# VectorE's side work ahead of both convolution taps, and the leftover gate product on VectorE, in a fused FNet mixing and gated convolution kernel

## The chip, the cores and the metric

The kernel runs on one core of a Trainium2 chip. A core has a matrix engine (TensorE, PE in the profile; its weight loads are listed as PEld), a vector engine (VectorE, DVE), an engine for functions of one operand (ScalarE, ACT), a general engine (GpSimd, POOL) and an engine that here only issues DMAs (SyncE, SP). Each runs its own list of instructions in order, and semaphores hold an instruction until what it reads or overwrites is ready. The metric is device time in microseconds (us) of one execution. Before the change three runs took 1197.53, 1198.07 and 1198.87 us; the median is 1198.07.

## What is computed

The input x has the shape (8, 3136, 256). A 2D Fourier transform over sequence and features, of which the real part is kept, is followed by a gated feed-forward layer with a three-tap convolution along the sequence:

```python
X = np.fft.fft(np.fft.fft(x, axis=1), axis=2).real      # (8, 3136, 256)
h = np.maximum(X @ w_in, 0.0)                           # (8, 3136, 1024)
hp = pad(h, 1 row of zeros at both ends of the sequence)
conv_out = sum(conv_w[k] * hp[:, k:k + S, :] for k in range(3))
gate = 1.0 / (1.0 + np.exp(-conv_out))
out = (h * gate) @ w_out                                # (8, 3136, 256)
```

All numbers are float32.

## The kernel before

**Stages.** The sequence transform of a batch is folded by symmetry on VectorE (`fold_ops`, 14 pieces per batch, L142 to L199), and multiplied with cosine and sine tables on PE in eight or nine "units" (`units`, L271 to L371). A unit has PE products into one PSUM bank, for most units a ScalarE copy of half of that bank into SBUF (`copy`, L286 for even frequencies, L305 for odd-even ones), and a `fin` on VectorE that adds and subtracts the two halves into the rows PQ of the transformed sequence (L290 and L293, L309 and L311; the units called `odd`, L321 and L323, have no copy, and their `fin` follows the PE products directly). The feature transform is merged with w_in into a matrix G, so the hidden rows come from two products of G with PQ.

**Steps.** The main loop runs over 256 steps (b, c, f): 8 batches, 4 chunks of the half sequence each, and 8 blocks of 128 hidden features. A step handles 128 features by 770 positions (832 in the last chunk of a batch), as two mirrored halves of some 385 columns. For each step there are:

- `seed`: ScalarE writes the contribution of one input feature into the PSUM tile pa.
- `products`: PE adds two products (pb, pa) of 386 to 418 columns (a third in some steps of batch 0, `triple`).
- `copies`: ScalarE copies pb to SBUF as nb (L685), in `triple` steps L680 and L682.
- `combine`: VectorE makes the hidden rows h from pa and nb (L696, two instructions, or one in `triple` steps).
- `first_tap`: ScalarE multiplies h with tap 0 into g (L702).
- `tap` 1 and 2: VectorE adds the two other taps into g, in place (L707, 128x770 or 128x832 each).
- `sigmoid`: ScalarE, two instructions on g (L720), the half for POOL first.
- `gate`: g times h, half on POOL (L727) and half on VectorE (L728). In the last chunk there are 64 more columns, left over from tiles of 128, that go into a tile `left` which two batches share; this is a third product, on POOL (L730).
- `mm2`: PE multiplies the gated tiles with w_out and adds over the eight f into the PSUM tiles po (six tiles, seven in the last chunk of odd batches, the seventh from `left`). At f = 7 ScalarE copies po out (L747) and SP stores it.

**Order.** The program order of each engine is written by hand. The loop at L893 runs cycles t = 0 to 258 and handles several steps at once: products for step t+1, `combine` and `first_tap` for step t, the two taps for step t-1, sigmoid and gate for step t-2, and `mm2` for step t-3. So step s is combined in cycle s and multiplied with w_out in cycle s+3. Work for the next batch and for loading is hung into the cycles as "side" work, by cycle and place: `first`, `act`, `dve`, `load` and `pe`. The place `dve` holds the fold pieces, the `fin` of units, parts of the conversion of the weights (L538, L539, L532, L542, up to cycle 7) and a stage of the transform of one feature (L449). The place `act` holds the units' copies and comes behind `copies` of step t+1 on ScalarE. VectorE's order in a cycle is therefore: conversion of weights where there is some (L524), combine (L696), tap 1, the `dve` side work, tap 2, gate.

A unit's PE products end in the cycle before its copy and `fin`. In batches 2 to 7 there is a unit about every four cycles, and fold pieces in other cycles; around cycles 21 to 29 units come in almost every cycle. Folding ends with batch 7's data, around cycle 190.

**Buffers.** One PSUM bank for pb, two for pa, one for the units (pd), four for po; four tiles h, five tiles g.

Of the kernel before, what the change touches and what calls it, by code (L numbers as in the profile page):

```python
# [13 lines left out]
ALU = mybir.AluOpType  # L14
# [23 lines left out]
def kernel(  # L38
# [48 lines left out]
    vt = nc.vector.tensor_tensor  # L87
    gt = nc.gpsimd.tensor_tensor
    stt = nc.vector.scalar_tensor_tensor
# [407 lines left out]
    LEFT = P // 2  # L497
# [4 lines left out]
    left = const.tile([P, NF, P], F32, name="left")  # L502
# [110 lines left out]
    cw = const.tile([P, 3, NF], F32, name="cw")  # L613
# [29 lines left out]
    def cut(s):  # L643
        b, c, f = s
        ch = chunks[c]
        return ch, ch.k1 - ch.k0, slice(f * P, (f + 1) * P)

    def seed(s):

        b, c, f = s  # L650
        ch, n, fs = cut(s)
        pa[s] = psa.tile([P, 512], F32, name="pa", tag="pa")
        act(pa[s][:, 0:n], eb[b, c], AF.Copy, scale=ge[:, f:f + 1])  # L653

    def triple(s):

        return s[0] == 0 and TRIPLE[0] <= s[1] * NF + s[2] < TRIPLE[1]

    def row_of(s):
        hs[s] = hp.tile([P, HW], F32, name="h", tag="h")  # L660
        w = chunks[s[1]].w
        if chunks[s[1]].zeros:
            nc.gpsimd.memset(hs[s][:, 0:w:w - 1], 0.0)  # L663

    def products(s):
        b, c, f = s
        ch, n, fs = cut(s)
        pb[s] = psb.tile([P, 512], F32, name="pb", tag="pb")
        mm(pb[s][:, 0:n], G[0:P - 1, 1, fs], PQ[b][1][0:P - 1, ch.k0:ch.k1], True, True)
        mm(pa[s][:, 0:n], G[:, 0, fs], PQ[b][0][:, ch.k0:ch.k1], False, not triple(s))  # L670
        if triple(s):
            mm(pa[s][:, 0:n], G[0:P - 1, 1, fs], PQ[b][1][0:P - 1, ch.k0:ch.k1], False, True)

    def copies(s):

        ch, n, fs = cut(s)
        p = pb.pop(s)
        nb[s] = nbp.tile([P, 2, HN], F32, name="nb", tag="nb")
        if triple(s):
            act(nb[s][:, 1, ch.cols], p[:, ch.cols], AF.Copy, scale=-2.0)  # L680
            row_of(s)
            act(hs[s][:, ch.front], pa[s][:, ch.fcols], AF.Relu)  # L682
        else:
            for i, cols in enumerate((ch.fcols, ch.cols)):
                act(nb[s][:, i, cols], p[:, cols], AF.Copy, scale=-1.0 if i else 1.0)  # L685

    def combine(s):

        ch, n, fs = cut(s)
        a, c = pa.pop(s), nb.pop(s)  # L690
        if not triple(s):
            row_of(s)
        h = hs[s]
        for i, (to, cols) in enumerate(((h[:, ch.front], ch.fcols), (h[:, ch.back][:, ::-1], ch.cols))):
            if i or not triple(s):
                nc.vector._custom_dve(TENSOR_ADD_SAT, out=to, in0=a[:, cols], in1=c[:, i, cols],  # L696
                                      s0=BIG, s1=0.0)

    def first_tap(s):
        n = chunks[s[1]].w - 2  # L700
        gs[s] = gp.tile([P, HW - 2], F32, name="g", tag="g")[:, 0:n]
        act(gs[s], hs[s][:, 0:n], AF.Copy, scale=cw[:, 0, s[2]:s[2] + 1])  # L702

    def tap(s, k):
        g, h, f = gs[s], hs[s], s[2]
        n = g.shape[1]
        stt(out=g, in0=h[:, k:k + n], scalar=cw[:, k, f:f + 1], in1=g, op0=ALU.mult, op1=ALU.add)  # L707

    def shares(s):

        ch = chunks[s[1]]
        w = ch.w - 2
        n = ch.rest[0] if ch.last else w
        return slice(0, n // 2), slice(n // 2, n), slice(n, w)

    def sigmoid(s):

        v, p, r = shares(s)
        for c in (slice(p.start, r.stop), v):
            act(gs[s][:, c], gs[s][:, c], AF.Sigmoid)  # L720

    def gate(s):

        b, c, f = s
        g, h = gs[s], hs.pop(s)[:, 1:]
        v, p, r = shares(s)
        gt(g[:, p], g[:, p], h[:, p], op=ALU.mult)  # L727
        vt(g[:, v], g[:, v], h[:, v], op=ALU.mult)  # L728
        if r.start < r.stop:
            gt(left[:, f, b % 2 * LEFT:(b % 2 + 1) * LEFT], g[:, r], h[:, r], op=ALU.mult)  # L730

    def mm2(s):
        b, c, f = s
        ch = chunks[c]
        tiles = [(gs[s][:, o:o + m], [(0, b, r, m)]) for o, r, m in ch.tiles]
        if ch.last and b % 2:
            tiles.append((left[:, f], [(i * LEFT, b - 1 + i, ch.rest[1], LEFT) for i in range(2)]))
        for i, (w, to) in enumerate(tiles):
            if f == 0 and i % 2 == 0:
                po[b, c, i // 2] = pso.tile([P, 2, D], F32, name="po", tag="po")  # L740
            pt = po[b, c, i // 2]
            mm(pt[:, i % 2, :], w, wout[:, f, :], f == 0 and i % 2 == 0, f == NF - 1)
            if f == NF - 1 and (i % 2 or i == len(tiles) - 1):
                del po[b, c, i // 2]
                osb = osp.tile([P, 2, D], F32, name="os", tag="os")
                for j in range(i - i % 2, i + 1):
                    nc.scalar.copy(out=osb[:, j % 2], in_=pt[:, j % 2])  # L747
                    for p0, b_, r, m in tiles[j][1]:
                        nc.sync.dma_start(out=rows[b_ * S + r:b_ * S + r + m, :], in_=osb[p0:p0 + m, j % 2])
        gs.pop(s)  # L750
# [49 lines left out]
    n = chunks[0].k1  # L800
# [9 lines left out]
    steps = [(b, c, f) for b in range(B) for c in range(len(chunks)) for f in range(NF)]  # L810
# [45 lines left out]
    for b in range(1, B):  # L856
        begin, us, *_ = units(b)
        us = us[0:4] + us[5:]
        c0, n = ends[b], per * b - 3 - ends[b]
        at(max(c0, per * (b - 1) + 1), "pe", begin)  # L860
        cs = [c0 + i * n // len(us) for i in range(len(us) + 1)]
        for i, u in enumerate(us):
            k = cs[i + 1] - cs[i]
# [8 lines left out]
    for b in range(1, B):  # L872
        ops = fold_ops(b)
        c0, n = ends[b - 1], ends[b] - ends[b - 1]
# [12 lines left out]
    n = len(steps)  # L887
# [5 lines left out]
    for t in range(n + LAG):  # L893
        def run(where):
            for fn in side.get((t, where), []):
                fn()
        if 0 <= t - 2 < n:
            sigmoid(steps[t - 2])
        run("first")
        if t + 1 < n:  # L900
            products(steps[t + 1])
            copies(steps[t + 1])
        run("act")
        if t < n:
            combine(steps[t])
        if t + 2 < n:
            seed(steps[t + 2])
        if t < n:
            first_tap(steps[t])

        if 0 <= t - 1 < n:
            tap(steps[t - 1], 1)
        run("dve")
        if 0 <= t - 1 < n:
            tap(steps[t - 1], 2)
        if 0 <= t - 2 < n:
            gate(steps[t - 2])
        run("load")
        if t >= LAG:
            mm2(steps[t - LAG])  # L920
        run("pe")
# [66 lines left out]
```

## Time and profile before

| quantity | value |
|---|---|
| median of three runs | 1198.07 us |
| the profiled execution: its own time | 1197.53 us |
| its span, from first to last instruction | 1195.8 us |
| instructions in it | 15377 |
| TensorE clock granted | 0.999 of full speed |
| tap, 128x770, VectorE L707 | 384 of 1.114 us in the mean |
| tap, 128x832, VectorE L707 | 128 of 1.184 us |
| hidden rows, VectorE L696 | 495 of 0.557 us |
| gate half on VectorE, L728 | 256 of 0.574 us |
| gate half on POOL, L727 | 256 of 1.047 us |
| leftover product on POOL, L730, 128x64 | 64 of 1.025 us (0.296 to 3.076) |
| output product on PE, po | 3072 instructions, 379 ns each as listed |

The page lists instructions by engine, line, operation and tiles ("out<-in"). "busy" is the time that the instructions of a group cover; a duration holds the way through the engine's pipeline, so two instructions that follow one another overlap by some 0.08 us, and what an instruction costs its engine is read from start to start. "idle before, releaser" is the time that the engine stood ahead of an instruction and whose work ended it. In a timeline row the first number is the start in us from the span's start, the second the duration, and "x2" stands for two instructions in a row that were merged. Instructions that only wait or branch aren't counted as busy. PE's busy time overstates its use, since its products are pipelined: two output products of 379 ns start 216 ns after each other.

### The profile page before, as it was taken

The page shows a single profiled execution, that of the slowest core. Times are in us where ns is not written, and L with a number is a line of the kernel's source. Part 1 is how long each engine was busy: PE and PEld are TensorE (multiplying, and loading weights), DVE is VectorE, ACT ScalarE, POOL GpSimd, SP SyncE. Part 2 cuts the span into 40 slices and gives each one's busy share as a digit, 9 for nine tenths or more (in the row PEclk, how much of TensorE's full clock was granted, in tenths as well). Part 3 has the DMA queues.
Part 4 walks back from the last instruction along what each step waited for, and adds up shares of the span by engine and source line. Part 5 has one row for each costly group of instructions (what it writes and reads, how often), then busy time and mean ns, then how long its engine had stood idle before and what let it go on. Part 6 is the DMA issues. An engine that isn't in the chain of part 4 may idle for free.

```text
span 1195.8 us, 15377 instructions
## 1 busy us (share of the span) xinstructions
PE 1169.0 (98%) x4836; PEld 901.1 (75%) x4836; DVE 1127.8 (94%) x1625; ACT 884.4 (74%) x1840; POOL 485.7 (41%) x540
## 2 busy tenths in 40 slices
PE   4999999999999999999999999999999999999998
PEld 2776777777777777777777777777777777777776
DVE  7899999999999999999999999999998988899996
ACT  2677667777777777777777777777776777788884
POOL 5235546454363433624345243632334222342224
PEclk9999999999999999999999999999999999999999
DMA  9812323212031211202021110310010100110000
GB/s 222 196 35 81 82 29 108 62 47 81 7 95 38 75 34 56 76 5 81 27 88 52 30 52 27 101 34 27 27 33 21 32 27 27 47 34 27 27 27 31
DMA packets 70067, 66.07 MB, mean 55 GB/s; under 512 B 28107, under 2 KB 57683, under 8 KB 69987
## 3 DMA queue, kind: packets, MB, share of 16 engines
q1 hardware_dynamic: 64349, 51.98, 15.4%
q0 software_dynamic: 5120, 12.85, 3.6%
q8 instruction: 38, 0.62, 0.2%
q10 hardware_dynamic: 518, 0.28, 0.1%
q14 instruction: 42, 0.34, 0.1%
HBM read 39.33 MB, written 25.74 MB: 54 GB/s over the span
## 4 chain that ended last, share of the span: by engine, by line
PE 84%; DVE 11%; issue 2%; ACT 1%; POOL 1%; DMA 0%; SPq 0%; ACTq 0%; DVEq 0%; POOLq 0%
PE po L93 51%; PE pb L93 13%; PE pa L93 12%; PE pd L93 8%; DVE g L707 5%; DVE h L696 1%; DVE g L728 1%; POOL xh L132 1%; DVE xh L157 0%; ACT nb L685 0%; DVE xh L168 0%; DVE w L186 0%; DVE wout L532 0%; ACT os L747 0%; DMA ed<-er 0%
## 5 line engine op out<-in xcount | busy, mean ns | idle before, releaser
L93 PE MATMUL po<-wout,g 128*128 128x256 f32 x3072 | 705.9, 379 | 5.1 <-DVE g L728 5.1
L93 PEld LDWEIGHTS po<-wout,g 128*128 128x128 f32 x3072 | 580.8, 190 | 149.4 <-issue 17.9
L707 DVE SCALAR_TENSOR_TENSOR g<-h,cw,g 128x770 f32<-128x770 f32 (+1 forms) x512 | 579.4, 1132 | 6.2 <-ACT g L702 2.4
L727 POOL TENSOR_TENSOR g<-g,h 128x385 f32<-128x385 f32 (+1 forms) x256 | 267.7, 1047 | 622.5 <-ACT g L720 429.6
L685 ACT ACTIVATE nb<-pb 128x386 f32<-128x386 f32 (+2 forms) x478 | 212.8, 499 | 163.3 <-PE pb L93 162.8
L720 ACT ACTIVATE g<-g 128x385 f32<-128x385 f32 (+2 forms) x512 | 245.0, 530 | 98.7 <-DVE g L707 96.8
L696 DVE CUSTOM_DVE_ANT_0 h<-pa,nb 128x386 f32<-128x386 f32 (+2 forms) x495 | 256.5, 557 | 3.1 <-POOL h L663 3.1
L702 ACT ACTIVATE g<-h,cw 128x770 f32<-128x770 f32 (+1 forms) x256 | 244.1, 954 | 0.0
L93 PE MATMUL pb<-qt,G 127*128 127x387 f32 (+2 forms) x512 | 212.8, 496 | 1.0 <-ACT G L622 1.0
L93 PE MATMUL pa<-pt,G 128*128 128x387 f32 (+2 forms) x512 | 211.8, 494 | 0.0
L653 ACT ACTIVATE pa<-eb,ge 128x387 f32<-128x387 f32 (+2 forms) x256 | 154.6, 604 | 0.8 <-ACT ft L458 0.6
L93 PEld LDWEIGHTS pa<-pt,G 128*128 128x128 f32 x512 | 96.8, 189 | 73.6 <-issue 17.9
L728 DVE TENSOR_TENSOR g<-g,h 128x385 f32<-128x385 f32 (+1 forms) x256 | 146.9, 574 | 3.5 <-ACT g L720 3.5
L93 PE MATMUL pd<-tab,w 98*128 98x196 f32 (+3 forms) x448 | 126.7, 374 | 0.0
L132 POOL DMA_INDIRECT xh<-in_x_dram,idx x64 | 106.4, 1662 | 13.3 <-issue 9.7
L93 PEld LDWEIGHTS pb<-qt,G 127*128 127x128 f32 x512 | 93.9, 190 | 19.1 <-ACT G L622 1.8
L93 PEld LDWEIGHTS pd<-tab,w 98*128 98x128 f32 (+1 forms) x448 | 84.7, 191 | 12.3
L730 POOL TENSOR_TENSOR left<-g,h 128x64 f32<-128x64 f32 x64 | 65.6, 1025 | 0.0
L747 ACT COPY os<-po 128x256 f32<-128x256 f32 x196 | 57.7, 392 | 9.8 <-DMA out_dram<-os 5.0
L187 POOL COPY w<-xh 98x4 f32<-98x4 f32 (+1 forms) x32 | 34.9, 1089 | 39.0 <-DVE xh L168 28.4
L157 DVE TENSOR_TENSOR xh<-xh 98x1020 f32<-98x1020 f32 (+1 forms) x32 | 39.5, 1239 | 2.4 <-DMA xh<-in_x_dram,idx 2.4
L168 DVE TENSOR_TENSOR xh<-xh 98x1024 f32<-98x1024 f32 (+1 forms) x32 | 39.0, 1217 | 0.1
(118 smaller groups left out, 363.4 us busy)
## 6 DMA issues: line engine op xcount, KB each, us to landing
out_dram<-os SPq DMA_DIRECT2D x192, 128.0 KB
xh<-in_x_dram SPq DMA_DIRECT2D x16, 784.0 KB
eb<-ed SPq DMA_DIRECT2D x16, 193.5 KB
tab<-dft_seq_dram SPq DMA_DIRECT2D x4, 589.5 KB
raw<-in_moe_w_in_dram SPq DMA_DIRECT2D x4, 512.0 KB
raw<-in_moe_w_out_dram SPq DMA_DIRECT2D x1, 2048.0 KB
eb<-ed SPq DMA_DIRECT2D x8, 209.0 KB
eb<-ed SPq DMA_DIRECT2D x7, 193.0 KB
```

Of the source, the lines that this page charges most:

```text
L93: nc.tensor.matmul(o, l, r, start=start, stop=stop, skip_group_check=True)
L132: nc.gpsimd.indirect_dma_start(out=xh[b, h][0:NP, 7 - m].rearrange("p q d -> p (q d)"), out_offset=None, in_=bass.AP(tensor=x.tensor, offs ...
L653: act(pa[s][:, 0:n], eb[b, c], AF.Copy, scale=ge[:, f:f + 1])
L685: act(nb[s][:, i, cols], p[:, cols], AF.Copy, scale=-1.0 if i else 1.0)
L696: nc.vector._custom_dve(TENSOR_ADD_SAT, out=to, in0=a[:, cols], in1=c[:, i, cols], s0=BIG, s1=0.0)
L702: act(gs[s], hs[s][:, 0:n], AF.Copy, scale=cw[:, 0, s[2]:s[2] + 1])
L707: stt(out=g, in0=h[:, k:k + n], scalar=cw[:, k, f:f + 1], in1=g, op0=ALU.mult, op1=ALU.add)
L720: act(gs[s][:, c], gs[s][:, c], AF.Sigmoid)
L727: gt(g[:, p], g[:, p], h[:, p], op=ALU.mult)
L728: vt(g[:, v], g[:, v], h[:, v], op=ALU.mult)
L730: gt(left[:, f, b % 2 * LEFT:(b % 2 + 1) * LEFT], g[:, r], h[:, r], op=ALU.mult)
L747: nc.scalar.copy(out=osb[:, j % 2], in_=pt[:, j % 2])
```

## The change

Two things are changed. The side work of the place `dve` moves ahead of tap 1, so that VectorE's order in a cycle becomes: combine, side work, tap 1, tap 2, gate; the function `tap` becomes `other_taps`, which issues both taps. And the leftover product of the last chunk moves from POOL to VectorE, where it comes right behind VectorE's half of the gate. The order of ScalarE, PE and SP is as before; POOL's is as before without the leftover products.

```diff
-    def tap(s, k):
+    def other_taps(s):
         g, h, f = gs[s], hs[s], s[2]
         n = g.shape[1]
-        stt(out=g, in0=h[:, k:k + n], scalar=cw[:, k, f:f + 1], in1=g, op0=ALU.mult, op1=ALU.add)
+        for k in (1, 2):
+            stt(out=g, in0=h[:, k:k + n], scalar=cw[:, k, f:f + 1], in1=g, op0=ALU.mult, op1=ALU.add)
...
         gt(g[:, p], g[:, p], h[:, p], op=ALU.mult)
         vt(g[:, v], g[:, v], h[:, v], op=ALU.mult)
         if r.start < r.stop:
-            gt(left[:, f, b % 2 * LEFT:(b % 2 + 1) * LEFT], g[:, r], h[:, r], op=ALU.mult)
+            vt(left[:, f, b % 2 * LEFT:(b % 2 + 1) * LEFT], g[:, r], h[:, r], op=ALU.mult)
...
         if t < n:
             combine(steps[t])
+        run("dve")
         if t + 2 < n:
             seed(steps[t + 2])
         if t < n:
             first_tap(steps[t])
-
-        if 0 <= t - 1 < n:
-            tap(steps[t - 1], 1)
-        run("dve")
         if 0 <= t - 1 < n:
-            tap(steps[t - 1], 2)
+            other_taps(steps[t - 1])
         if 0 <= t - 2 < n:
             gate(steps[t - 2])
```

## The prediction

> **What bounds the kernel now.** I read the page's busy shares and chain first, then busy time by stretch, then the waits, then the timeline around the moved work.
>
> ```profile
> PE 1169.0 (98%) x4836; PEld 901.1 (75%) x4836; DVE 1127.8 (94%) x1625; ACT 884.4 (74%) x1840; POOL 485.7 (41%) x540
> ...
> PE 84%; DVE 11%; issue 2%; ACT 1%; POOL 1%; DMA 0%; SPq 0%; ACTq 0%; DVEq 0%; POOLq 0%
> ```
>
> TensorE (PE) sets the end for most of the span; VectorE (DVE) is hardly less busy and holds 11% of the chain. By stretch (columns: length, then busy of PE, PEld, DVE, ACT, POOL):
>
> ```profile
> 44.00:238.00 194.00, 188.58 (x775) 139.69 (x776) 190.19 (x271) 138.89 (x303) 91.23 (x103) 1.00 0.32 70
> 238.00:910.00 672.00, 671.66 (x2785) 523.53 (x2784) 645.08 (x949) 515.00 (x1059) 279.80 (x296) 1.00 0.16 50
> 910.00:1196.00 286.00, 280.92 (x1164) 219.53 (x1162) 257.64 (x345) 217.47 (x452) 91.20 (x102) 1.00 0.09 29
> ```
>
> Three regimes: early, VectorE is never idle for long and PE waits for it; in the middle PE is full and VectorE has 4% over; late, VectorE has room. The waits that matter (us in total, times, longest):
>
> ```profile
> PEld po L93 <- DVE g L728: 15.6, 21, 2.4
> DVE pt L290 <- ACT as L286: 13.6, 13, 2.1
> DVE qt L290 <- ACT as L286: 12.5, 13, 2.1
> ...
> DVE as L309 <- ACT as L305: 8.0, 9, 2.5
> ```
>
> VectorE's spare time is spent in one place: before the "fin" of a DFT unit (L290, L309), until ScalarE's copy of that unit's PSUM has come. There VectorE is brought back in step with PE. VectorE in one such cycle (start, duration):
>
> ```profile
> 548.83 1.21 DVE L707 SCALAR_TENSOR_TENSOR g<-h,cw,g 128x770 f32<-128x770 f32 x1
> 551.01 0.52 DVE L290 TENSOR_TENSOR qt<-as,pd 128x196 f32<-128x196 f32 x1 [0.97 <-ACT as L286]
> 551.36 0.53 DVE L293 TENSOR_TENSOR qt<-pd,as 128x196 f32<-128x196 f32 x1
> 551.74 0.98 DVE L707 SCALAR_TENSOR_TENSOR g<-h,cw,g 128x770 f32<-128x770 f32 x1
> 552.65 0.54 DVE L728 TENSOR_TENSOR g<-g,h 128x385 f32<-128x385 f32 x1
> ```
>
> ScalarE's copy ran from 550.65 to 550.98, so the first tap (548.83) lies inside the time that VectorE waits anyway. The gate product ends at 553.19; PE's next output product, which reads it, starts at 554.58. I call this distance the margin, here 1.39 us, and read it so from the timeline for every cycle t of the loop at L893 (this one is t = 109). At zero margin PE stands: at cycle 95 the gate ended at 493.78 and PE started at 493.83, 0.33 late against its rhythm, so PE waits once the margin would fall under 0.05.
>
> **The change part by part.**
>
> *Taps behind the side work.* Nothing is removed from VectorE; on ScalarE, POOL and SP the order stays (POOL's row copies L187 follow the same VectorE products, no DMA issue is passed). Three costs:
>
> (a) Behind a wait. 42 fins wait for a ScalarE copy, and in 40 of them the copy ended 0.6 to 3.5 us after the start of the first tap. With the fin ahead, the whole first tap runs after the copy: tap, second tap, gate and the next hidden states (L696) queue behind it, and PE and ScalarE's sigmoid wait for them.
>
> (b) Back to back. The second tap reads what the first wrote. Apart, a tap lets the next instruction start 0.93 later (551.74 to 552.65 is 0.91); a pair takes longer:
>
> ```profile
> 50.89 2.07 DVE L707 SCALAR_TENSOR_TENSOR g<-h,cw,g 128x770 f32<-128x770 f32 x2
> 52.87 0.42 DVE L524 TENSOR_SCALAR wout<-raw 128x512 int32<-128x512 int32 x1
> ```
>
> 1.98 against 2 x 0.93: 0.12 more. Today about 148 cycles have side work between the taps and escape it; afterwards none does. So (a) is 0.93 + 0.12 = 1.05 per waiting fin, and each further cycle with side work adds 0.12 until the next wait sets VectorE back in step.
>
> (c) ScalarE. Once VectorE is over some 0.6 late, the sigmoid ends after PE's product and pushes ScalarE's next copies, and so the next fin, by the excess.
>
> *Leftover product from POOL to VectorE.* 64 instructions of 128x64, in the eight steps of each last chunk. VectorE has no such row; the nearest start-to-start times are 0.084 (L160, 98x8) and 0.47 (L728, 128x385: 552.65 to 553.12). On the line between them 64 columns cost 0.14; bounds 0.084 and 0.47, so 5 to 30 us of VectorE, 9.0 taken. [...] Only where the margin is gone does this reach PE. POOL's saving of 64 x 1.03 us counts nothing: PE waits for none of it, and the 17 taps beside that product alone were 4 ns longer. In odd batches PE's last pair reads the leftover 2.6 us after the first: covered.
>
> **Sum, early (44 to 238 us).** Cycle 2: L532 already waits 1.09 for ScalarE's L526 behind its first tap, so the tap falls behind the wait: 1.05. Cycles 3 to 20, 15 with side work: 15 x 0.12 = 1.8; VectorE never idles there and margins at cycles 17 to 19 are 0.05, so both reach PE. Cycles 23 to 29 have fins in almost every cycle, so (c) adds up: lateness 1.7 at 24 against margin 1.27 (loss 0.48), 0.18 at 28, and at 29 (margin 0.06) 0.78 of later copy plus a tap of 1.08: 1.84. Cycles 30 to 37, margins about 0.05: 8 x 0.12 + 5 leftovers x 0.14 = 1.65. Together 7.0.
>
> **Sum, middle (238 to 910).** Loss = lateness - what is already lost since the last fin - margin + 0.05. Batch 2:
>
> | cycle | margin | lateness | loss |
> |---|---|---|---|
> | 74 | 1.18 | 1.05+0.12 | 0.04 |
> | 79 | 0.91 | 1.05+2x0.12 | 0.43 |
> | 89 | 1.43 | 1.05+0.55 (c) | 0.22 |
> | 90 | 1.00 | 1.72 | 0.55 |
> | 94 | 0.96 | 1.05+0.30 (c)+0.12+0.14 | 0.70 |
> | 95 | -0.28 | 1.61+0.12+0.14 | 1.50, 0.33 of it there today |
>
> 3.1 us. Batch 4 has the same margins to 0.1: 3.1. Batch 3 has 0.43, 0.77 and, at cycle 127 (margin 1.00, lateness 1.57), 0.62: 1.9. Batch 1 (cycles 46, 50, 58, 59, 63; the last two 0.76 and 0.86): 2.0. Batch 5, where folding ends: 1.3. Elsewhere margins of 1.5 to 4 cover it. Together 11.4.
>
> **Late:** smallest margin at a fin 1.1 (cycle 221) against 1.05, then growing: 0.
>
> Sum 18.4. The profiled execution took 1197.53 (span 1195.8 and 1.7 around it), 0.5 under the median of 1198.07: 1215.9, say 1216.
>
> **An unknown: collisions with POOL.** A tap that starts just behind POOL's gate product stands until it is done; so do other VectorE products of two SBUF operands:
>
> ```profile
> 191.82 1.77 DVE L707 SCALAR_TENSOR_TENSOR g<-h,cw,g 128x832 f32<-128x832 f32 x1
> 191.83 0.87 POOL L727 TENSOR_TENSOR g<-g,h 128x384 f32<-128x384 f32 x1
> ...
> 387.64 1.66 POOL L727 TENSOR_TENSOR g<-g,h 128x385 f32<-128x385 f32 x1 [3.28 <-ACT g L720]
> 388.49 1.36 DVE L172 TENSOR_TENSOR xh<-xh 98x512 f32<-98x512 f32 x1
> ```
>
> 1.77 where 1.08 is usual, 1.36 where 0.68 is. First taps with side work behind them lose 9.9 us so in the early stretch, 9.1 outside fins (8.0 in the middle, outside fins). Now a folding product follows L696 instead. I take it to inherit the loss (0 saved), by the row of L172; the other end is all of it saved. [...]
>
> **The rivals.**
>
> *Forecast, 0.60:* 1216. By itself 1207 (half of the collisions saved) to 1225: the leftover at 0.47 adds 0.33 on some 13 places on the path, 4 us, and (c), 4 to 5 us of the sum, may be twice as large.
>
> *Margins hold in the middle, 0.22:* if ScalarE's copies come a little earlier or lateness doesn't add up, only the early stretch pays: 1197.5 + 7.0 = 1204.5. For it: 672 us with PE full and margins of 1 to 3. Against: margins 0.91 and -0.28 are under 1.05 alone.
>
> *VectorE becomes the bound of the middle, 0.10:* ScalarE hands the lateness on from fin to fin. At 1.05 for each of the middle's 30 fins that wait for a copy, nothing absorbed, 1197.5 + 7.0 + 31 = 1235. Against: before every middle fin VectorE has 1.2 to 2.6 us between L696's end and the copy, which absorbs most.
>
> *Not slower, 0.08: the collisions vanish.* Place: the slot behind L696 in side cycles. Saved early 9.1, so early 7.0 - 9.1 = -2.1. In the middle the tight cycles carry the largest collisions (59, 63, 95, 127: 0.52 to 0.70 each) and 0.12 in the mean elsewhere, which cancels (b): the same table then gives 0.3, 0.9, 0.3, 0.9, 0.3, together 2.8. 1198.2, no change. It decides only when nearly all of it is saved; half of it leaves 1207.
>
> **How the numbers follow.** A measurement of this kernel can tell about 0.2% (2.4 us) from no change. The range takes the forecast's own bounds, reaches to the cheap case and leaves out the collision case and most of the dear one: 1203 to 1226. Chances: slower 0.91 (forecast, cheap, dear, and the upper side of the collision case), no change 0.05, faster 0.04 (both from the collision case).
>
> **What would show it.** Waits of VectorE at L290 and L309 up from 34 to 60 us or more; PE's waits for the gate product up by some 15; PE no longer full between 470 and 500 and between 750 and 790; the lines of the taps always in pairs; the leftover on VectorE at about 0.22 long, 0.14 to the next start. Wrong if PE's waits for VectorE in the middle stay near zero, or if the folding products behind L696 keep their 1.13 while early taps become short.

## The result, and the profile after

The changed kernel takes 1211.66 us (median of four runs, 1210.64 to 1212.37) against 1197.89 us before (median of four, one run more than above): a ratio of 1.0113, 95% interval 1.0095 to 1.0131, slower by some 13.8 us. The forecast was 1216, in a range of 1203 to 1226. The profiled execution has a span of 1209.3 us, 13.5 more than before.

Busy time and the chain that ended last, from the page of the changed kernel:

```profile
PE 1176.9 (97%) x4836; PEld 899.1 (74%) x4836; DVE 1120.2 (93%) x1689; ACT 882.6 (73%) x1840; POOL 374.0 (31%) x476
...
PE 70%; DVE 22%; issue 4%; ACT 2%; POOL 1%; DMA 1%; DVEq 0%; SPq 0%; POOLq 0%; ACTq 0%
```

VectorE's share of the chain went from 11% to 22%, though VectorE is busy for 7.6 us less than before and has 64 instructions more. In sum VectorE has no more work than before; its work comes later. Busy time by stretch (length, then PE, PEld, DVE, ACT, POOL):

```profile
44.00:238.00 194.00, 184.77 (x754) 135.53 (x755) 186.30 (x273) 135.70 (x296) 70.96 (x92) 1.00 0.31 70
238.00:910.00 672.00, 668.92 (x2750) 515.00 (x2749) 633.87 (x971) 506.35 (x1045) 211.24 (x259) 1.00 0.16 49
910.00:1209.00 299.00, 294.47 (x1219) 229.86 (x1217) 265.81 (x387) 227.88 (x471) 68.43 (x86) 1.00 0.10 30
```

In the middle stretch PE, which had been full, executes 35 products fewer in the same 672 us, and VectorE is busy 11 us less. The waits say for what (us in total, times, longest):

```profile
ACT g L721 <- DVE g L708: 192.2, 174, 3.2
ACT nb L685 <- PE pb L93: 83.1, 105, 1.6
PEld po L93 <- DVE g L729: 45.8, 78, 2.6
...
DVE qt L290 <- ACT as L286: 20.2, 14, 3.1
...
DVE pt L290 <- ACT as L286: 19.3, 14, 3.3
...
DVE as L309 <- ACT as L305: 16.0, 15, 3.2
```

VectorE's waits for the units' copies are 55.5 us instead of 34.1, and PE's weight loads wait 45.8 us in 78 places for VectorE's gate product, instead of 15.6 in 21. ScalarE's sigmoid now waits 192.2 us for VectorE's taps (96.8 before) and its copies 83.1 us for PE (162.8 before): ScalarE, which had waited for PE, waits for VectorE. The cycle shown of before (t = 109) is now, on VectorE:

```profile
557.57 1.02 DVE L696 CUSTOM_DVE_ANT_0 h<-pa,nb 128x386 f32<-128x386 f32 x2
560.15 0.53 DVE L290 TENSOR_TENSOR qt<-as,pd 128x196 f32<-128x196 f32 x1 [1.57 <-ACT as L286]
560.50 0.54 DVE L293 TENSOR_TENSOR qt<-pd,as 128x196 f32<-128x196 f32 x1
560.86 2.07 DVE L708 SCALAR_TENSOR_TENSOR g<-h,cw,g 128x770 f32<-128x770 f32 x2
562.85 0.55 DVE L729 TENSOR_TENSOR g<-g,h 128x385 f32<-128x385 f32 x1
```

The wait is 1.57 long instead of 0.97, both taps stand behind it (1.99 from start to the next start), and the gate ends at 563.40. PE's output product, which reads it, starts at 563.72: the margin is 0.32 where it was 1.39. The exposed tap cost 1.07; the prediction had 1.05. The next cycles' margins were 1.22 and 0.91 and are now 0.05, the least at which PE starts: there it waited.

Where PE lost its time, by the start of the same cycle's first product in both traces:

| stretch (cycles) | forecast | PE later by |
|---|---|---|
| up to cycle 3, mostly DMAs at the start | 0 | 0.5 |
| 3 to 38 (early, with cycle 2's wait) | 7.0 | 4.5 |
| 38 to 190 (middle) | 11.4 | 8.3 |
| 190 to the end | 0 | 0.2 |
| sum | 18.4 | 13.5 |

Of the signs that the prediction named, the waits for the copies rose to 55.5 us and not to 60, and PE's waits for the gate product by 30 us and not by 15; PE executes 122 products instead of 125 between 470 and 500 us, and 162 instead of 165 between 750 and 790; all 256 pairs of taps stand together. One sign of being wrong came in part: the first taps of cycles 3 to 37 take 36.4 us in sum instead of 46.2, and the folding products only 4.4 us more (44.4 instead of 40.0). The term on collisions with POOL was thus partly wrong; it is taken up below.

### The profile page after: what moved, and what is told of

Read it like the earlier page. It is cut to its first block, busy times and chain, and to the rows that moved or that the text cites. A ratio compares the mean times of both kernels' runs of the same rounds, so it can differ in the third digit from the quotient of the medians.

```text
span 1209.3 us, 15374 instructions
## 1 busy us (share of the span) xinstructions
PE 1176.9 (97%) x4836; PEld 899.1 (74%) x4836; DVE 1120.2 (93%) x1689; ACT 882.6 (73%) x1840; POOL 374.0 (31%) x476
## 4 chain that ended last, share of the span: by engine, by line
PE 70%; DVE 22%; issue 4%; ACT 2%; POOL 1%; DMA 1%; DVEq 0%; SPq 0%; POOLq 0%; ACTq 0%
PE po L93 43%; PE pb L93 11%; PE pa L93 10%; DVE g L708 7%; PE pd L93 6%; DVE h L696 3%; DVE g L729 3%; DVE xh L157 2%; ACT nb L685 1%; DVE xh L168 1%; DVE w L185 1%; POOL xh L132 1%; DVE w L186 1%; DMA xh<-in_x_dram 0%; DVE pt L290 0%
## 5 line engine op out<-in xcount | busy, mean ns | idle before, releaser
L93 PEld LDWEIGHTS po<-wout,g 128*128 128x128 f32 x3072 | 578.4, 189 | 164.9 <-DVE g L729 45.8
L708 DVE SCALAR_TENSOR_TENSOR g<-h,cw,g 128x770 f32<-128x770 f32 (+1 forms) x512 | 548.6, 1072 | 9.3 <-ACT g L702 0.2
L728 POOL TENSOR_TENSOR g<-g,h 128x385 f32<-128x385 f32 (+1 forms) x256 | 233.9, 914 | 758.2 <-ACT g L721 502.7
L721 ACT ACTIVATE g<-g 128x385 f32<-128x385 f32 (+2 forms) x512 | 244.6, 528 | 194.7 <-DVE g L708 192.2
L685 ACT ACTIVATE nb<-pb 128x386 f32<-128x386 f32 (+2 forms) x478 | 210.7, 493 | 84.2 <-PE pb L93 83.1
L696 DVE CUSTOM_DVE_ANT_0 h<-pa,nb 128x386 f32<-128x386 f32 (+2 forms) x495 | 257.1, 560 | 0.0
L93 PEld LDWEIGHTS pa<-pt,G 128*128 128x128 f32 x512 | 96.8, 189 | 73.6 <-issue 18.6
L132 POOL DMA_INDIRECT xh<-in_x_dram,idx x64 | 105.8, 1653 | 13.3 <-issue 9.2
L157 DVE TENSOR_TENSOR xh<-xh 98x1020 f32<-98x1020 f32 (+1 forms) x32 | 40.7, 1279 | 2.6 <-DMA xh<-in_x_dram,idx 2.6
L168 DVE TENSOR_TENSOR xh<-xh 98x1024 f32<-98x1024 f32 (+1 forms) x32 | 41.7, 1302 | 0.1
L187 POOL COPY w<-xh 98x4 f32<-98x4 f32 (+1 forms) x32 | 19.6, 611 | 26.8 <-DVE xh L168 14.8
L290 DVE TENSOR_TENSOR qt<-as,pd 128x197 f32<-128x197 f32 (+1 forms) x14 | 7.3, 518 | 20.2 <-ACT as L286 20.2
```

The lines of the kernel that those rows point to most:

```text
L93: nc.tensor.matmul(o, l, r, start=start, stop=stop, skip_group_check=True)
L132: nc.gpsimd.indirect_dma_start(out=xh[b, h][0:NP, 7 - m].rearrange("p q d -> p (q d)"), out_offset=None, in_=bass.AP(tensor=x.tensor, offs ...
L157: vt(a[:, :, :, 1:D], a[:, :, :, 1:D], r[:, :, :, D - 1:0:-1], op=ALU.add)
```

## Experiments

Theory A is the forecast's: the first tap used to lie inside VectorE's wait for the unit's copy, now it comes behind it, and on top the taps follow back to back; PE's margins take this up until they are used up. Rival B: the 64 leftover products on VectorE cost the time. Rival C: the pairs of taps and the folding's new place cost it, not the wait. "Shift" below is the delay of PE against the kernel before, by cycle as in the table above.

### The order alone

```diff
-            vt(left[:, f, b % 2 * LEFT:(b % 2 + 1) * LEFT], g[:, r], h[:, r], op=ALU.mult)
+            gt(left[:, f, b % 2 * LEFT:(b % 2 + 1) * LEFT], g[:, r], h[:, r], op=ALU.mult)
```

(on the changed kernel)

> The side work goes ahead of both taps, the leftover product stays on POOL. Theory A (the first tap comes out from under VectorE's wait for ScalarE's copy, and the taps follow back to back): nearly the whole loss, 11 to 13 us, 1209 to 1211. Rival B (the 64 leftover products on VectorE are what costs, 14 us of busy time at 0.22 us each): at most 2 us over the kernel before, under 1200.

Measured: 1212.74 us, ratio 1.0123 (1.0106 to 1.0140), above the 1209 to 1211 that were expected; shift 4.6 early, 9.5 in the middle. The order alone costs the whole loss, or a little more than the whole change: the two intervals overlap, so the leftover's effect within the new order can't be told from nothing by the times. Rival B is out.

### The leftover alone

```diff
-            gt(left[:, f, b % 2 * LEFT:(b % 2 + 1) * LEFT], g[:, r], h[:, r], op=ALU.mult)
+            vt(left[:, f, b % 2 * LEFT:(b % 2 + 1) * LEFT], g[:, r], h[:, r], op=ALU.mult)
```

(on the kernel before; the runs below with "the leftover on VectorE" build on this one)

> The order stays as before, only the leftover product goes to VectorE. Theory A: 0 to 2 us more than before, 1198 to 1200, since the product reaches PE only in the few cycles without margin. Rival B: 8 us or more, over 1206. If POOL's leftover products had been what lengthened the taps, the taps' mean falls from 1.13 us; if it was POOL's gate product alone, it stays.

Measured: 1199.48 us, ratio 1.0008 (0.9998 to 1.0018), shift 1.3 early and -0.4 in the middle. As theory A has it. The taps' mean (128x770) is 1.113 us against 1.114, so POOL's leftover product had not been what lengthened them.

### Only the fins ahead

```diff
-            at(cs[i + 1], "dve", u.fin)
+            at(cs[i + 1], "fin", u.fin)
...
             combine(steps[t])
+        run("fin")
...
             tap(steps[t - 1], 1)
         run("dve")
         if 0 <= t - 1 < n:
             tap(steps[t - 1], 2)
```

(with the leftover on VectorE; `fin` is a new place for side work)

> With the leftover on VectorE: only the fins of the DFT units go ahead of both taps, the folding, the weight pieces and the feature stage stay between the taps. Theory A, part a (behind a wait): most of the loss in the middle stretch, 6 to 9 us over the run with the leftover alone, 1205 to 1208; VectorE's waits at L290 and L309 near 55 us. Rival C (the back-to-back taps and the folding's new place cost, not the wait): at most 2 us over it.

Measured: 1205.87 us, ratio 1.0065 (1.0048 to 1.0081): 6.4 us over the leftover alone. Its waits at the fins:

```profile
DVE qt L290 <- ACT as L286: 20.9, 14, 3.2
DVE pt L290 <- ACT as L286: 20.9, 14, 3.3
DVE as L309 <- ACT as L305: 15.3, 15, 3.2
```

57 us, as in the changed kernel. Shift 2.6 early, 4.1 in the middle. The fin's place alone brings about half of the loss: against rival C.

### Only the rest ahead

```diff
             combine(steps[t])
+        run("dve")
...
             tap(steps[t - 1], 1)
-        run("dve")
+        run("fin")
         if 0 <= t - 1 < n:
             tap(steps[t - 1], 2)
```

(with the leftover on VectorE, and the fins in the place `fin` as above)

> With the leftover on VectorE: folding, weight pieces and feature stage go ahead of both taps, the fins stay between the taps. Theory A: 2 to 5 us over the run with the leftover alone (1.05 in cycle 2, 0.12 for each pair of taps where VectorE bounds), 1201 to 1204, waits at L290 and L309 near the 34 us of before. Rival C: 8 us or more, over 1206.

Measured: 1200.35 us, ratio 1.0013 (1.0003 to 1.0023), 0.9 over the leftover alone, which is less than expected and, by the intervals, not clear of nothing; shift 2.3 early and -0.6 in the middle. The two halves together make 6.4 + 0.9 = 7.3 us, the full change some 12. The rest is in neither alone. I read it so: the fin in front takes 1.07 of a margin of 0.9 to 1.4, and only then do the 0.12 of each pair and the folding's lateness meet PE, so losses behind a margin don't add up like durations. No run takes this last step apart.

### The copy earlier, in the changed kernel

```diff
-            at(cs[i + 1], "act", u.copy)
+            at(cs[i + 1], "first", u.copy)
```

> The changed kernel, but ScalarE makes each unit's copy ahead of the copies of the next step's product (place first instead of act), so that it is ready when VectorE comes to the fin. Theory A (the wait for the copy is the cause in the middle): VectorE's waits at L290 and L309 fall from 55 us to under 15, PE's shift between 238 and 910 us falls from 8 us to under 2, and the time to 1202 to 1206; what is left is the early stretch. If lateness came from the taps' pairs and the folding's place as such, the time stays over 1208.

Measured: 1199.17 us, ratio 1.0012 (1.0002 to 1.0022). One place of a ScalarE instruction, and the loss against the kernel before is gone but for about 1 us; that is less than the 1202 to 1206 that were expected. Shift in the middle -0.7; early 1.6. Waits:

```profile
PEld po L93 <- DVE g L729: 16.1, 20, 1.7
...
DVE as L309 <- ACT as L305: 7.9, 6, 2.3
DVE qt L290 <- ACT as L286: 6.9, 7, 1.7
...
DVE pt L290 <- ACT as L286: 5.0, 5, 1.7
```

19.8 us at the fins (under 15 was expected), and PE's waits for the gate are those of before, 16.1 in 20 places. VectorE's order, the pairs and the leftover are those of the changed kernel. So the wait for the copy is the cause of most of the loss. The fair comparison for what is left is the kernel before with the same earlier copy, the next run: it took 1197.06 us beside this one, so the new order and the leftover still cost 2.1 us when the copy is early, of the 13.8.

### The copy earlier, in the kernel before

The same edit on the kernel before, twice:

> The kernel before, with the same earlier copy on ScalarE. Theory A: VectorE's 34 us of waits at L290 and L309 mostly go, and the time stays within 2 us of before, 1196 to 1199, since they were covered by the margin to PE. If those waits had cost PE time, 1190 or less.

> The same kernel as the one before with the earlier copy, in more rounds. Theory A: it takes away PE's 0.3 us losses in the two cycles without margin and no more, 0.5 to 1.5 us below before.

Measured: 1197.06 us, ratio 0.9988 (0.9979 to 0.9998), and 1197.13 us, 0.9989 (0.9980 to 0.9998). The waits at the fins fall from 34.1 to 8.6 us (first of the two) and the time by 1 us or a little more. In both traces PE gains 0.44 to 0.45 at each of cycles 31, 97 and 161, just behind places without margin; two places with 0.3 were expected. This version is 0.1% under the kernel before, by intervals that only just leave 1 out, and some 1.2% under the changed one. So 25 us of VectorE's waiting went for 1 us of the kernel's time. Not all of it became free time on VectorE: the taps take 591.0 us in sum instead of 579.4 and the folding products 145.6 instead of 137.8, which I read as more of them standing behind POOL.

### The side work behind both taps

```diff
             tap(steps[t - 1], 1)
-        run("dve")
-        if 0 <= t - 1 < n:
             tap(steps[t - 1], 2)
+        run("dve")
```

(with the leftover on VectorE)

> With the leftover on VectorE: both taps ahead of the side work, so back to back in every cycle as in the changed kernel, but with no tap behind a wait. Theory A: the pairs alone cost only where VectorE is the bound (15 cycles early at 0.12, some 2 us), the middle nothing: within 3 us of the run with the leftover alone, 1198 to 1202. Rival C (the pairs are the cause): 1206 or more.

Measured: 1200.68 us, ratio 1.0023 (1.0013 to 1.0032). Pairs in every cycle, no tap behind the wait: about 0.15% over the leftover alone. Together with the run "Only the rest ahead", where the folding's new place and its pairs cost 0.9 us, this puts rival C out.

### The wait alone, in the old order

```diff
-            at(cs[i + 1], "act", u.copy)
+            at(cs[i + 1], "dve", u.copy)
```

(on the kernel before; the copy then comes behind seed and first tap on ScalarE)

> The kernel before (order of VectorE and leftover as before), but ScalarE makes each unit's copy only behind the seed (0.6 us) and the first tap (0.94 us), so 1.5 us later: the wait alone, with no other change. Theory A: like a longer form of the changed kernel's exposed tap (1.05 us); waits at L290 and L309 rise from 34 to some 90 us, PE is late by 8 to 13 us between 238 and 910 us, in all 1207 to 1212. And if it is VectorE's lateness that keeps the first taps clear of POOL's gate product, the taps' mean (128x770) falls below 1.09 us from 1.11 though the order is that of before. If the change's loss hung on the order of the instructions and not on the wait, the time stays under 1202.

Measured: 1220.98 us, ratio 1.0192 (1.0175 to 1.0210), shift 4.6 early, 15.6 in the middle: more than the 1207 to 1212 that were expected. The waits at the fins are 77 us (some 90 expected). PE also has a new wait that I had not seen coming:

```profile
PE pd L93 <- DVE qt L293: 4.0, 14, 0.7
PE pd L93 <- DVE pt L293: 3.0, 9, 0.3
...
PE pd L93 <- DVE as L311: 2.4, 5, 0.5
```

The fins now end so late that the next unit's products wait for the one PSUM bank, 9.4 us in sum; that these waits make up the excess is likely, but not shown. The taps' mean is 1.096 us, lower than 1.114 but not under the 1.09 that was named: lateness frees some of the taps from POOL, not all that the change freed (1.060). What stands: in the old order, with nothing on VectorE moved, a later copy slows the kernel in the same way, so it is the wait and not the order as such.

## Why the prediction was right

**What bounds, and the mechanism.** As foreseen: PE waits for the gate in the cycles that follow a fin, the late stretch pays nothing, and taking the wait away takes the loss away. Of the rivals, the margins did not hold in the middle (8.3 us were lost there), and VectorE did not become its bound (that would have cost 31 us). The fourth rival's condition came true in good part. Early, the first taps shed nearly all of their collisions, and the folding products took on about half of that (the sums are given above). In the middle, the first taps of cycles 38 to 189 take 156.4 us in sum instead of 173.7, and the folding products took on almost none of that (93.4 instead of 93.0). Its price did not: it gave 1198 for all of them saved and 1207 for half. In the middle, 12 of these 17 us fall into cycles that had a margin over 1.2, such as cycle 91 below, where PE gains nothing, and a pair behind a fin takes its full 1.99. The forecast had set the saving to nothing without weighing this cover, so that it came as near as 4.3 us is in part luck.

**(a), the tap behind the wait:** 1.05 forecast, 1.07 measured (cycles 73, 77, 105, 109: margins of 1.39 to 1.40 became 0.32 to 0.35).

**(b), the pairs:** 1.99 from the first tap's start to the gate's, against 2 x 0.93: 0.13, forecast 0.12.

**The leftover:** 0.218 us long and 0.13 to 0.14 from start to start, forecast 0.22 and 0.14. The length of 0.22 was an estimate of mine that no row of the kernel before shows; the 64 products on VectorE took 0.210 to 0.223. What VectorE gave up was not their length but the distance of the starts, 0.14 us. With the leftover alone PE was 1.3 us later early and not later in the middle.

**Cycle 2 and cycles 23 to 29:** cycle 2 cost 0.67 (forecast 1.05), cycles 3 to 21 1.5 (1.8), cycles 23 to 29 2.3 (2.5). In cycle 2 the wait for ScalarE's L526 is 2.03 instead of 1.09.

**What was too large,** 18.4 against 13.5, is mostly one term: "I take it to inherit the loss (0 saved)", of the collisions with POOL. It failed first at the end of the first five batches: in cycles 31, 63, 95, 127 and 159 the first tap took 1.75 to 1.92 before and takes 1.08 now. In cycle 95, where the forecast had 1.17 more of loss, the kernel before has:

```profile
485.96 3.24 POOL L132 DMA_INDIRECT xh<-in_x_dram,idx  x1 [0.19 <-issue]
...
489.23 0.88 POOL L727 TENSOR_TENSOR g<-g,h 128x384 f32<-128x384 f32 x1
489.24 1.76 DVE L707 SCALAR_TENSOR_TENSOR g<-h,cw,g 128x832 f32<-128x832 f32 x1
```

and the changed kernel:

```profile
494.20 2.87 POOL L132 DMA_INDIRECT xh<-in_x_dram,idx  x1 [0.18 <-issue]
...
497.83 1.08 DVE L696 CUSTOM_DVE_ANT_0 h<-pa,nb 128x418 f32<-128x418 f32 x2
498.07 0.86 POOL L728 TENSOR_TENSOR g<-g,h 128x384 f32<-128x384 f32 x1 [1.00 <-issue]
498.83 1.21 DVE L157 TENSOR_TENSOR xh<-xh 98x1020 f32<-98x1020 f32 x1
```

POOL's gate product runs beside L696; only its last 0.10 overlaps the folding product. L696, which reads pa from PSUM and nb from SBUF, takes 1.08 with it and took 1.08 before without it (from 488.24 on), and the folding product behind it takes its plain 1.21. Before, POOL came to this product only when the gather of the cycle before (L132, which issues an indirect DMA) was done, at 489.20, just when the first tap started. That gather starts behind the leftover product as long as POOL has it. The runs tell the two parts of the change apart here. With the leftover alone the tap still takes 1.75 in cycle 95. With the order alone, the leftover still on POOL, the folding product inherits part of the loss:

```profile
496.05 1.65 POOL L132 DMA_INDIRECT xh<-in_x_dram,idx  x1 [0.18 <-issue]
...
497.73 0.88 POOL L728 TENSOR_TENSOR g<-g,h 128x384 f32<-128x384 f32 x1
498.21 1.55 DVE L157 TENSOR_TENSOR xh<-xh 98x1020 f32<-98x1020 f32 x1
```

L157 takes 1.51 to 1.56 so in cycles 63, 95, 127 and 159. With only the rest ahead and the leftover on VectorE it takes 1.21 in all four, though VectorE is not late there (31 us of waits at the fins, shift -0.6 in the middle). Lateness alone doesn't do it: with the late copy in the old order the tap still takes 1.75 to 1.92 in all five cycles, and with only the fins ahead 1.76 to 1.93 in three of them and 1.08 in cycles 95 and 159. So what frees all five is the side work ahead together with the leftover's leaving POOL, whose saving the prediction had counted as nothing. Why the gather takes 2.87 in one run and 4.46 with the leftover alone no run here shows.

Elsewhere in the middle, lateness does it. In cycle 91 the first tap took 1.60 before; it takes 1.07 now and 1.10 with the late copy in the old order, but 1.39 with only the rest ahead, where VectorE is on time. ScalarE's waits fit this: in the mean of the middle the sigmoid starts 0.06 behind the second tap's end instead of 0.27, and POOL's product 0.72 behind it instead of 0.97. But cycle 91 had a margin of 1.25, so there PE had nothing to gain. The taps of the middle stretch (238 to 910 us), before:

```profile
L707 DVE SCALAR_TENSOR_TENSOR g<-h,cw,g 128x770 f32<-128x770 f32 x228 | 244.4, 1072 | 1.3 <-ACT g L702 0.2
L707 DVE SCALAR_TENSOR_TENSOR g<-h,cw,g 128x832 f32<-128x832 f32 x76 | 87.9, 1156 | 0.5
```

and after:

```profile
L708 DVE SCALAR_TENSOR_TENSOR g<-h,cw,g 128x770 f32<-128x770 f32 x232 | 237.8, 1025 | 4.1
L708 DVE SCALAR_TENSOR_TENSOR g<-h,cw,g 128x832 f32<-128x832 f32 x70 | 75.4, 1078 | 1.2
```

0.047 and 0.078 shorter, on some 230 and 73 of them about 16 us. Over the whole run the taps of the changed kernel are 27 us shorter than with the leftover alone (548.6 against 575.8), the folding's products (L157, L168, L172, L185, L186) only 6 longer (142.3 against 136.0). With only the fins ahead, where VectorE is late and the folding stays in its place, the taps are 14 us shorter (561.8) and the folding products 3 (133.5).

Where VectorE is on time, the folding inherits most of it. With only the rest ahead, the taps lose 19 us (556.8) and the folding takes on 13 (149.4). Its two dearest rows, first with the leftover alone, then with the rest ahead:

```profile
L168 DVE TENSOR_TENSOR xh<-xh 98x1024 f32<-98x1024 f32 (+1 forms) x32 | 38.9, 1215 | 0.1
L157 DVE TENSOR_TENSOR xh<-xh 98x1020 f32<-98x1020 f32 (+1 forms) x32 | 38.5, 1209 | 2.5 <-DMA xh<-in_x_dram,idx 2.5
```

```profile
L168 DVE TENSOR_TENSOR xh<-xh 98x1024 f32<-98x1024 f32 (+1 forms) x32 | 42.1, 1316 | 0.1
L157 DVE TENSOR_TENSOR xh<-xh 98x1020 f32<-98x1020 f32 (+1 forms) x32 | 40.8, 1280 | 2.7 <-DMA xh<-in_x_dram,idx 2.7
```

A folding product that starts just behind POOL's gate product thus inherits the loss, as the prediction took it from its row of L172: L157 at 498.21 above ends 1.15 behind the end of POOL's product, about its usual 1.21 later, and in the changed kernel L168 at 95.87, beside POOL's product of 95.66 to 96.52, takes 1.74, where the same piece took 1.21 before (at 95.02). What the forecast lacked was that both the lateness and POOL's shorter list change who starts when.

The same shows term by term. In batch 2 the losses were 0.21 (forecast 0.04) behind cycle 74, 0.67 (0.43) behind 78 and 79, 0.36 (0.77) at 89 and 90, and 0.75 (1.87) at 94 and 95. Cycles 30 to 37, 1.65 in the forecast, cost nothing on balance: the first taps of cycles 31 and 33 are 0.84 and 0.58 shorter, and at cycles 33 and 34 the margins were 0.79 and 0.21, not the 0.05 that the forecast took for all of them. Term (c), too, came only in the run of units around cycle 24: at cycle 89 the margin lost 1.12 and not 1.60, since the lateness had gone down to 0.24 by cycle 88, where L172 had collided before.

How the 13.5 us divide between pairs, folding and saved collisions in each cycle is worked out from two traces, not measured one by one; that hardly a collision is left of the middle's first taps is read from their durations, and a run that changes only POOL's moment wasn't made.

## What to carry to other kernels

A wait that an engine has anyway is a place to hide work: ask of each instruction that is moved across a wait whether it lay inside it, for then the whole of it comes out on the other side. Compare that with the margin of the consumer, cycle by cycle, and not with busy shares: here PE's margins were 0.9 to 1.4 us, the exposed tap 1.07, and small costs that had cover before (0.12 for a pair) seem to count once the margin is gone: the two halves of the order cost 7.3 us apart and some 12 together. Where an order must put a waiting instruction first, make its producer earlier: one copy ahead of another on ScalarE was worth 12 us.

## What was not expected of the hardware

That the change freed VectorE of some 21 us of standing behind POOL (taps 27 us less, folding 6 more), though no instruction was changed but in its place, and the leftover in its engine. Lateness accounts for the larger part: with only the fins ahead VectorE gains some 16.5 us so. Where it fell into covered cycles, it was worth nothing to PE; where it counted, in the last cycle of a batch, it took the leftover's leaving POOL as well. And that a copy 1.5 us later cost 22 us, where 1 us of exposed tap had cost 12: with the late copy the units' one PSUM bank became a second wait, of PE on VectorE, 9.4 us in sum.
